# V's weights in whole rows by contraction blocks, and a new order of the first V projections, in a one-core attention and gated-MLP kernel

## The chip, the cores and the metric

The kernel runs on one core of a Trainium2 chip. The metric is the device time of one execution in microseconds. The time is the median of the runs; beside it stands one execution that was taken with the hardware profiler, from which all rows and durations come.

## The reference

One input x (2048 rows of 640) goes through a layer norm, and the normalised rows feed two branches whose results are added to x:

```python
xn = _layernorm(x)
# A: 32 heads of 20, a causal window of 256
qkv = (xn @ wqkv).reshape(B, S, 3, H, Dh)          # wqkv: 640 x 1920
scores = einsum("bhqd,bhkd->bhqk", q, k) * Dh**-0.5
p = softmax(where(0 <= i - j < 256, scores, -1e9))
A = (p @ v) @ wo                                    # wo: 640 x 640
# B: a gated unit
Bo = (sigmoid(xn @ w_gate) * (xn @ w_up)) @ w_down  # 640 x 1536, 1536 x 640
return x + A + Bo
```

All tensors are bfloat16.

## The kernel before

The 2048 rows are worked in four chunks of 512 rows, each of four blocks of 128 (`s` is the block in the chunk, 0 to 3). The 640 features are five contraction blocks of 128 (`d`, 0 to 4). A normalised block is turned (rows to columns) so that the features lie on the partitions, in `xnT`. Everything after the first V projections runs from an order written out by hand: TensorE is fed with scores and with pieces of the other matmuls from a list. The change touches only the start, chunk 0, up to the first matmul of Q.

**Transfers at the start.** They all go out on SP's queue, in program order: the blocks 0, 1 and 3 of x, the first half of V's weights, block 2 of x, the second half of V's weights, then Q's, K's and the gated unit's weights. V's weights are the last 640 columns of `wqkv`, held in SBUF as `wqkv[2]`, 128 partitions by 5 contraction blocks by 640. A half is 320 columns of all five contraction blocks, so each row that it reads in HBM is 640 bytes. A DMA runs on 16 DMA engines, and its reader waits for the last of them.

**Layer norm of the first four blocks.** `ln_block` (bn_stats on two halves, then the aggregate, L252 and L258) with `root` (ACT's square root, L649) and `norm` (DVE's reciprocal L653 and normalisation L271) is the way over DVE. `mean_act`, `root_act` and `norm_act` (L659, L664, L665, L669, L670) take the mean and the squares on ACT, and only the last two small steps on DVE. Before, blocks 0 and 3 go over DVE, blocks 1 and 2 over ACT.

**Transposes.** `transpose_rows(s, copy)` has TensorE transpose a block's five 128 x 128 squares into one PSUM buffer `pt` (L277), and `copy` (ACT's or DVE's) brings them to `xnT[0]` (L278). Block 0 is copied by ACT in two pieces, contraction blocks 0 to 2 and 3 to 4.

**V.** `project_v(c, s, hf)` sums five matmuls of 128 x 320 (L353) into a PSUM buffer `pv`: block s, half hf of V's columns. Its name below is `v` with s and hf: `v10` is block 1, first half. `between` is a function that is called after the third matmul, which puts other work for TensorE there. `copy_v` brings a finished sum to the V tile in two copies (L364), by ACT or by DVE; `proj_v` does both. There are two PSUM pools of four buffers each: `ps_d` (sums) and `ps_h` (transposes, and block 3's two sums).

**Keeping TensorE busy.** `keep_busy` (L226) issues matmuls of ones that nobody reads.

Each engine works through its instructions in program order, so the order of the calls in the start section (L673 to L711) is the order on TensorE, ACT and DVE. After V come the five blocks of Q and the five of K (`g_qk(0)`, L324), and the gated unit's and scores' matmuls. Q's results leave PSUM by DVE, K's by ACT (L328, L330).

Of the kernel before, what the change touches and what calls it, by code (L numbers as in the profile page):

```python
# [9 lines left out]
P = 128  # L10
S = 2048
D = 640
# [3 lines left out]
DC = D // P  # L16
FC = F // P
CW = 512
# [7 lines left out]
HALF = 320  # L26
# [12 lines left out]
FP32 = mybir.dt.float32  # L39
# [54 lines left out]
def kernel(  # L94
# [11 lines left out]
    nc = tc.nc  # L106
# [4 lines left out]
    def pool(name, bufs, **kw):  # L111
        return ctx.enter_context(tc.tile_pool(name=name, bufs=bufs, **kw))
# [15 lines left out]
    ps_d = pool("ps_d", 4, space=bass.MemoryType.PSUM)  # L128
    banks = ctx.enter_context(ExitStack())
    ps_h = banks.enter_context(tc.tile_pool(name="ps_h", bufs=4, space=bass.MemoryType.PSUM))  # L130
# [11 lines left out]
    wqkv = [const.tile([P, DC + (part != "v"), D], BF16, name="w" + part) for part in "qkv"]  # L142
    wqkv_r = A_wqkv.rearrange("(c p) n -> p c n", p=P)
# [6 lines left out]
    def load_wqkv(part):  # L150
        nc.sync.dma_start(out=wqkv[part][:, 1:, :], in_=wqkv_r[:, :, part * D:(part + 1) * D])
# [3 lines left out]
    def load_rows(s, queue):  # L155
        queue.dma_start(out=xc[0][:, s, :], in_=xr[:, s, :])  # L156

    def load_v(hf):
        a = hf * HALF
        nc.sync.dma_start(out=wqkv[2][:, :, a:a + HALF], in_=wqkv_r[:, :, 2 * D + a:2 * D + a + HALF])  # L160

    load_rows(0, nc.sync)
    load_rows(1, nc.sync)
    load_rows(3, nc.sync)
    load_v(0)
    load_rows(2, nc.sync)
    load_v(1)
    load_wqkv(0)
    load_wqkv(1)

# [78 lines left out]
    def ln_half(c, s, a, stats=None):  # L249
        if a == 0:  # L250
            stats = lnp.tile([P, 2, nc.vector.BN_STATS_DIM], FP32, name="stats")
        nc.vector.bn_stats(out=stats[:, a, :], in_=xc[c][:, s, a * HALF:(a + 1) * HALF])  # L252
        return stats

    def ln_mv(stats, mv=None):
        if mv is None:
            mv = lnp.tile([P, nc.vector.BN_AGGR_DIM], FP32, name="mv")
        nc.vector.bn_aggr(out=mv, in_=stats)  # L258
        return mv

    def ln_block(c, s, mv=None):
        return ln_mv(ln_half(c, s, 1, ln_half(c, s, 0)), mv)
# [7 lines left out]
    def norm_block(c, s, mv, rstd):  # L270
        nc.vector.tensor_scalar(out=xns[c][:, s, :], in0=xc[c][:, s, :], scalar1=mv[:, 0:1],  # L271
                                scalar2=rstd[:, 0:1], op0=SUB, op1=MULT)

    def transpose_rows(s, copy, lo=0, hi=DC):
        pt = ps_h.tile([P, DC, P], BF16, name="pt", tag="h")
        for d in range(lo, hi):
            nc.tensor.transpose(pt[:, d, :], xns[0][:, s, d * P:(d + 1) * P], ident)  # L277
        copy(out=xnT[0][:, lo:hi, s * P:(s + 1) * P], in_=pt[:, lo:hi, :])  # L278
# [68 lines left out]
        nc.gpsimd.memset(v[:, :, 0:16 * VW].rearrange("p k (h d) -> p k h d", d=VW)[:, :, :, DH:VW], 0.5)  # L347
        nc.gpsimd.memset(v[:, :, 16 * VW:], 0.0)

    def project_v(c, s, hf, home=ps_d, tag="d", between=None):  # L350
        ps = home.tile([P, CW], FP32, name="pv", tag=tag)
        for d in range(DC):
            nc.tensor.matmul(ps[:, 0:HALF], lhsT=xnT[c][:, d, s * P:(s + 1) * P],  # L353
                             rhs=wqkv[2][:, d, hf * HALF:(hf + 1) * HALF],
                             start=(d == 0), stop=(d == DC - 1))
            if between and d == 2:
                between()
        return ps

    def copy_v(c, s, hf, ps, copy, us=(0, 1)):  # L360

        v = vt[c * SBC + s][hf * U:(hf + 1) * U, :, 0:16 * VW].rearrange("p k (h d) -> p k h d", d=VW)
        for u in us:
            copy(out=v[:, u, :, 0:DH],  # L364
                 in_=ps[u * U:(u + 1) * U, 0:HALF].rearrange("p (h d) -> p h d", d=DH))

    def proj_v(c, s, hf, copy):
        copy_v(c, s, hf, project_v(c, s, hf), copy)
# [278 lines left out]
    def root(mv):  # L647
        r = lnp.tile([P, 1], FP32, name="rstd")
        nc.scalar.activation(out=r, in_=mv[:, 1:2], func=SQRT, bias=eps)  # L649
        return r  # L650

    def norm(s, mv, r):
        nc.vector.reciprocal(r, r)  # L653
        norm_block(0, s, mv, r)

    def mean_act(s):
        xn = xns[0][:, s, :]
        neg = lnp.tile([P, 1], FP32, name="neg")
        nc.scalar.activation(out=xn, in_=xc[0][:, s, :], func=IDENTITY, scale=-1.0 / D, accum_out=neg)  # L659
        return xn, neg  # L660

    def root_act(s, xn, neg):
        r = lnp.tile([P, 1], FP32, name="rstd")
        nc.scalar.activation(out=xn, in_=xc[0][:, s, :], func=SQUARE, bias=neg, accum_out=r)  # L664
        nc.scalar.activation(out=r, in_=r, func=SQRT, bias=eps, scale=1.0 / D)  # L665
        return r

    def norm_act(s, xn, neg, r):
        nc.vector.reciprocal(r, r)  # L669
        nc.vector.tensor_scalar(out=xn, in0=xc[0][:, s, :], scalar1=neg[:, 0:1],  # L670
                                scalar2=r[:, 0:1], op0=ADD, op1=MULT)
# [5 lines left out]
    act, dve = nc.scalar.copy, nc.vector.tensor_copy  # L677
# [8 lines left out]
    keep_busy((CW, P))  # L686
    norm_act(1, xn1, neg1, r1)
    mv3 = ln_mv(ln_half(0, 3, 1, stats3))
    transpose_rows(1, dve)
    v00 = project_v(0, 0, 0)  # L690
    r3 = root(mv3)
    xn2, neg2 = mean_act(2)
    r2 = root_act(2, xn2, neg2)
    norm(3, mv3, r3)
    v10 = project_v(0, 1, 0)
    copy_v(0, 0, 0, v00, dve, (0,))
    transpose_rows(3, dve)
    v01 = project_v(0, 0, 1)
    norm_act(2, xn2, neg2, r2)
    copy_v(0, 0, 0, v00, act, (1,))  # L700
    copy_v(0, 1, 0, v10, act)
    v11 = project_v(0, 1, 1)
    copy_v(0, 0, 1, v01, act)
    v30 = project_v(0, 3, 0, ps_h, "h", lambda: transpose_rows(2, dve))
    copy_v(0, 3, 0, v30, act)
    v31 = project_v(0, 3, 1, ps_h, "h")
    copy_v(0, 1, 1, v11, dve)
    copy_v(0, 3, 1, v31, act)
    proj_v(0, 2, 0, dve)
# [75 lines left out]
    c = NCH - 1  # L785
# [64 lines left out]
```

## Time and profile before

| what | us |
|---|---|
| median of 3 runs (307.92 to 308.11) | 308.0 |
| the profiled execution | 308.12 |
| its span | 306.4 |
| TensorE's granted clock, share of full | 1.00 |
| V's first matmul (L353) starts | 7.10 |
| Q's first matmul (L324) starts | 13.09 |

The span is the time from the first to the last instruction that the profile shows; the execution's own time has 1.7 us more around it. Times in the timeline and in the chain are microseconds from the start of the span. A line of the timeline is a start, a length, the engine, the line of the kernel, the operation, what it writes and reads with its shape, how many instructions are merged, and in brackets the idle time ahead of it with what ended it. PE is TensorE, PEld its weight loads, DVE VectorE, ACT ScalarE, POOL GpSimd, SPq the queue that issues DMAs.

### The profile page before, as it was taken

The numbers are of one execution on the slowest core, as the hardware profiler recorded it, in microseconds if no ns is written. First come the engines' busy times: TensorE is split into PE (matmuls) and PEld (weight loads), VectorE is DVE, ScalarE is ACT, GpSimd is POOL, SyncE is SP. The second block draws the span as 40 slices with busy tenths as digits, with TensorE's granted clock in tenths as the row PEclk, the third lists the DMA queues.
The fourth block names the chain that finished last, engine by engine and source line by source line (L and its number), as shares of the span: only waits on it lengthen the run. The fifth ranks groups of instructions, "written<-read, shape, count | busy, mean of one in ns | idle before, by whom it ended". The sixth has DMA issues, their size and how long they took to land.

```text
span 306.4 us, 10016 instructions
## 1 busy us (share of the span) xinstructions
PE 299.8 (98%) x4290; PEld 165.4 (54%) x4325; DVE 177.6 (58%) x355; ACT 199.2 (65%) x198; POOL 177.0 (58%) x317
## 2 busy tenths in 40 slices
PE   7999999999999999999999999999999999999996
PEld 3654444445657654554557654554546665444775
DVE  5735539879675564496946464483733626372434
ACT  6933877698854649888674647878585547778000
POOL 3174687687982927676682728557382847657000
PEclk9999999999999999999999999999999999999999
DMA  7997977886427052810046212740000210000202
GB/s 204 364 328 259 300 201 220 313 242 203 156 90 171 21 181 68 263 50 2 2 132 131 66 58 71 249 142 0 2 2 2 68 43 25 2 2 2 88 21 68
DMA packets 40174, 36.87 MB, mean 120 GB/s; under 512 B 8864, under 2 KB 39840, under 8 KB 40096
## 3 DMA queue, kind: packets, MB, share of 16 engines
q1 hardware_dynamic: 39264, 35.46, 37.6%
q10 hardware_dynamic: 864, 0.75, 0.8%
q8 instruction: 34, 0.56, 0.7%
q14 instruction: 12, 0.10, 0.1%
HBM read 25.59 MB, written 11.44 MB: 121 GB/s over the span
## 4 chain that ended last, share of the span: by engine, by line
PE 96%; DMA 2%; issue 1%; SPq 0%; ACT 0%; ACTq 0%; DVE 0%
PE y L472 18%; PE pu L456 17%; PE pg L449 17%; PE pqk L324 14%; PE ps L529 9%; PE pv L353 7%; PE y L480 7%; PE acc L562 6%; DMA wv<-in_A_wqkv_dram 2%; SPq L156 0%; ACT th L821 0%; PE pt L277 0%; ACTq L496 0%; DVE xn L484 0%
## 5 line engine op out<-in xcount | busy, mean ns | idle before, releaser
L546 POOL TENSOR_SCALAR_AFFINE_SELECT pT<-pT 64x512 bf16<-64x512 bf16 (+1 forms) x256 | 157.0, 613 | 83.4 <-ACT pT L535 71.0
L535 ACT ACTIVATE pT<-ps 128x2048 bf16<-128x2048 f32 (+1 forms) x76 | 141.0, 1855 | 59.4 <-PE ps L529 58.7
L460 DVE SCALAR_TENSOR_TENSOR h<-th,pu 128x512 bf16<-128x512 f32 x48 | 32.7, 680 | 49.8 <-PE pu L456 44.2
L456 PE MATMUL pu<-xnT,wu 128*128 128x512 bf16 x228 | 59.0, 380 | 0.7 <-issue 0.2
L449 PE MATMUL pg<-xnT,wg 128*128 128x512 bf16 x226 | 58.5, 380 | 1.0 <-issue 0.3
L472 PE MATMUL y<-wd,h 128*128 128x320 bf16 (+3 forms) x407 | 56.6, 292 | 0.0
L472 PEld LDWEIGHTS <-h 128*128 128x128 bf16 x407 | 37.1, 98 | 15.3 <-issue 1.8
L452 ACT ACTIVATE th<-pg 128x512 f32<-128x512 f32 x48 | 28.6, 595 | 15.5 <-PE pg L449 15.4
L449 PEld LDWEIGHTS <-wg 128*128 128x128 bf16 x240 | 22.2, 98 | 25.8 <-issue 1.8
L456 PEld LDWEIGHTS <-wu 128*128 128x128 bf16 x240 | 22.0, 98 | 25.5 <-issue 2.0
L529 PE MATMUL ps<-qT,kT 20*64 20x320 bf16 (+4 forms) x1440 | 32.1, 260 | 0.0
L574 DVE STREAM_TRANSPOSE t<-acc 128x512 f32<-128x512 f32 x32 | 21.1, 697 | 17.3 <-PE acc L562 17.3
L529 PEld LDWEIGHTS <-kT 20*64 20x64 bf16 x1440 | 15.4, 103 | 25.0 <-issue 22.4
L484 DVE SCALAR_TENSOR_TENSOR rows<-y,rows 128x320 bf16<-128x320 f32 x30 | 14.5, 487 | 22.9 <-PE y L480 22.7
L586 DVE TENSOR_TENSOR on<-t,rec 128x320 bf16<-128x320 f32 (+4 forms) x48 | 26.0, 542 | 1.1
L353 PE MATMUL pv<-wv,xnT 128*128 128x320 bf16 x160 | 25.6, 300 | 0.1
L480 PE MATMUL y<-wo,oc 128*128 128x320 bf16 (+2 forms) x165 | 24.2, 295 | 0.0
L324 PE MATMUL pqk<-xnT,wk 128*128 128x512 bf16 x97 | 23.0, 380 | 0.2
L324 PE MATMUL pqk<-xnT,wq 128*128 128x512 bf16 x94 | 22.7, 380 | 0.4 <-issue 0.2
L364 DVE CAST v<-pv 64x320 bf16<-64x320 f32 x29 | 14.1, 485 | 11.7 <-PE pv L353 11.4
L562 PE MATMUL acc<-pT,v 64*32 64x320 bf16 (+4 forms) x1440 | 19.7, 253 | 0.0
L562 PEld LDWEIGHTS <-v 64*32 64x32 bf16 x1440 | 16.2, 91 | 5.8 <-issue 1.6
(54 smaller groups left out, 195.4 us busy)
## 6 DMA issues: line engine op xcount, KB each, us to landing
qT<-sq SPq DMA_DIRECT2D x16, 256.0 KB
kT<-sk SPq DMA_DIRECT2D x16, 256.0 KB
sq<-st SPq DMA_DIRECT2D x20, 128.0 KB
sk<-st SPq DMA_DIRECT2D x20, 128.0 KB
out_dram<-rows SPq DMA_DIRECT2D x15, 160.0 KB
wg<-in_B_w_gate_dram SPq DMA_DIRECT2D x4, 480.0 KB
wu<-in_B_w_up_dram SPq DMA_DIRECT2D x4, 480.0 KB
xc<-in_A_x_dram SPq DMA_DIRECT2D x3, 640.0 KB
```

The costliest lines, as they stand in the source:

```text
L324: nc.tensor.matmul(ps, lhsT=wt[:, m, :], rhs=xnT[c][:, d, :], start=(d == 0), stop=(d == DC - 1))
L353: nc.tensor.matmul(ps[:, 0:HALF], lhsT=xnT[c][:, d, s * P:(s + 1) * P], rhs=wqkv[2][:, d, hf * HALF:(hf + 1) * HALF], start=(d == 0), stop ...
L449: nc.tensor.matmul(pg, lhsT=part(wg, d, f), rhs=xnT[c][:, d, :], start=(d == 0), stop=(d == DC - 1))
L452: nc.scalar.activation(out=th, in_=pg, func=TANH, scale=0.5)
L456: nc.tensor.matmul(pu, lhsT=part(wu, d, f), rhs=xnT[c][:, d, :], start=(d == 0), stop=(d == DC - 1))
L460: nc.vector.scalar_tensor_tensor(out=h, in0=th, scalar=1.0, in1=pu, op0=ADD, op1=MULT)
L472: nc.tensor.matmul(y[:, lo:lo + width], lhsT=ht[c, f][:, s * P:(s + 1) * P], rhs=wd[:, f, cut[0] + lo:cut[0] + lo + width], start=(f == 0) ...
L480: nc.tensor.matmul(y[:, 0:cut[1] - cut[0]], lhsT=oc[c, m][:, s * P:(s + 1) * P], rhs=wo[:, m, cut[0]:cut[1]], start=False, stop=(m == DC - 1))
L529: nc.tensor.matmul(ps[a * U:(a + 1) * U, i, col * U:(col + n) * U], lhsT=qk["k", kc, o // GH][32 * i:32 * i + DH, o % GH + a, kb * U:(kb + ...
L535: nc.scalar.activation(out=pt[:, :, 0:width], in_=ps[:, :, 0:width], func=EXP, scale=SCALE)
L546: nc.gpsimd.affine_select(out=view, in_=view, pattern=[[0, HG], [0, n], [sign, U]], compare_op=GE, fill=0.0, base=base, channel_multiplier ...
L562: nc.tensor.matmul(acc[32 * i:32 * i + 32, q * U:(q + n) * U], lhsT=vt[kb][a * U:(a + 1) * U, u, h * VW:h * VW + 32], rhs=pt[a * U:(a + 1) ...
```

## The change

V's weights are loaded as contraction blocks 0 to 2 and then 3 to 4, each in whole rows of 640 columns (1280 bytes), and block 2 of x follows both pieces. TensorE begins both sums of block 0 before either is complete: three matmuls of `v00` come ahead of block 1's transposes, three of `v01` behind them, then the remaining two of each. Block 3's transposes stand after two matmuls of `v10` and are copied by ACT. Block 2's layer norm goes over DVE (`ln_block`, `root`, `norm`), its transposes stand after one matmul of `v31`. ACT takes both copies of `v00`. All of V's sums and all copies are still made once.

```diff
-    def load_v(hf):
-        a = hf * HALF
-        nc.sync.dma_start(out=wqkv[2][:, :, a:a + HALF], in_=wqkv_r[:, :, 2 * D + a:2 * D + a + HALF])
+    def load_v(lo, hi):
+        nc.sync.dma_start(out=wqkv[2][:, lo:hi, :], in_=wqkv_r[:, lo:hi, 2 * D:])
...
-    load_v(0)
+    load_v(0, 3)
+    load_v(3, DC)
     load_rows(2, nc.sync)
-    load_v(1)
...
-    def project_v(c, s, hf, home=ps_d, tag="d", between=None):
-        ps = home.tile([P, CW], FP32, name="pv", tag=tag)
-        for d in range(DC):
+    def add_v(ps, c, s, hf, lo, hi):
+        for d in range(lo, hi):
             nc.tensor.matmul(ps[:, 0:HALF], lhsT=xnT[c][:, d, s * P:(s + 1) * P],
                              rhs=wqkv[2][:, d, hf * HALF:(hf + 1) * HALF],
                              start=(d == 0), stop=(d == DC - 1))
-            if between and d == 2:
-                between()
+
+    def project_v(c, s, hf, home=ps_d, tag="d", between=None, at=0):
+        ps = home.tile([P, CW], FP32, name="pv", tag=tag)
+        add_v(ps, c, s, hf, 0, at)
+        if between:
+            between()
+        add_v(ps, c, s, hf, at, DC)
         return ps
...
+    v00 = ps_d.tile([P, CW], FP32, name="pv", tag="d")
+    v01 = ps_d.tile([P, CW], FP32, name="pv", tag="d")
+    add_v(v00, 0, 0, 0, 0, 3)
     transpose_rows(1, dve)
-    v00 = project_v(0, 0, 0)
+    add_v(v01, 0, 0, 1, 0, 3)
+    add_v(v00, 0, 0, 0, 3, DC)
+    add_v(v01, 0, 0, 1, 3, DC)
     r3 = root(mv3)
-    xn2, neg2 = mean_act(2)
-    r2 = root_act(2, xn2, neg2)
     norm(3, mv3, r3)
-    v10 = project_v(0, 1, 0)
-    copy_v(0, 0, 0, v00, dve, (0,))
-    transpose_rows(3, dve)
-    v01 = project_v(0, 0, 1)
-    norm_act(2, xn2, neg2, r2)
-    copy_v(0, 0, 0, v00, act, (1,))
+    mv2 = ln_block(0, 2)
+    copy_v(0, 0, 0, v00, act)
+    v10 = project_v(0, 1, 0, between=lambda: transpose_rows(3, act), at=2)
+    r2 = root(mv2)
+    v11 = project_v(0, 1, 1)
+    norm(2, mv2, r2)
+    copy_v(0, 0, 1, v01, act)
     copy_v(0, 1, 0, v10, act)
-    v11 = project_v(0, 1, 1)
-    copy_v(0, 0, 1, v01, act)
-    v30 = project_v(0, 3, 0, ps_h, "h", lambda: transpose_rows(2, dve))
+    v30 = project_v(0, 3, 0, ps_h, "h")
+    v31 = project_v(0, 3, 1, ps_h, "h", lambda: transpose_rows(2, dve), 1)
     copy_v(0, 3, 0, v30, act)
-    v31 = project_v(0, 3, 1, ps_h, "h")
     copy_v(0, 1, 1, v11, dve)
     copy_v(0, 3, 1, v31, act)
     proj_v(0, 2, 0, dve)
     proj_v(0, 2, 1, act)
```

## The prediction

> **What bounds the kernel now.** I read the page first (shares, then the chain), then the chain in order of time, then the timeline of the first 16 us engine by engine, then the packet and completion records of the first transfers.
>
> The page's first part and its chain:
>
> ```profile
> PE 299.8 (98%) x4290; PEld 165.4 (54%) x4325; DVE 177.6 (58%) x355; ACT 199.2 (65%) x198; POOL 177.0 (58%) x317
> PE 96%; DMA 2%; issue 1%; SPq 0%; ACT 0%; ACTq 0%; DVE 0%
> ```
>
> TensorE carries 96% of the chain. The one other piece of size is a DMA, 2%. The chain in order of time (start, length, what) shows where that lies:
>
> ```profile
> 2.18 4.88 DMA wv<-in_A_wqkv_dram
> 7.06 0.04 issue
> 7.10 1.52 PE pv L353 x10
> 8.62 0.28 PE pt L277 x5
> 8.90 1.77 PE pv L353 x13
> 10.66 0.28 PE pt L277 x5
> 10.94 2.31 PE pv L353 x17
> 13.25 0.21 PE pqk L324
> ```
>
> The first half of V's weights lands at 7.06 us; from 7.10 TensorE runs without a hole until Q's first matmul starts at 13.09 (the timeline's figure; the chain books it later since matmuls overlap). That stretch is 40 matmuls of V at 0.136 (5.43) and 10 transposes at 0.056 (0.56): 5.99 us, no stall in it. After it TensorE stays packed to the end, so whatever moves Q's first matmul moves the end by as much, and nothing after V in this diff can win time. The timeline gives what surrounds it (start, length, engine, line):
>
> ```profile
> 5.77 0.75 ACT L278 COPY xnT<-pt 128x384 bf16<-128x384 bf16 x2
> 6.53 0.45 PE L277 MATMUL pt<-ident,xn 128*128 128x128 bf16 x5 [0.41 <-DVE xn L670]
> 7.04 0.48 DVE L278 COPY xnT<-pt 128x640 bf16<-128x640 bf16 x1
> 7.48 0.16 DVE L653 RECIPROCAL rstd<-rstd 128x1 f32<-128x1 f32 x1
> 7.68 0.45 DVE L271 TENSOR_SCALAR xn<-xc,mv,rstd 128x640 bf16<-128x640 bf16 x1
> 9.64 4.79 ACT L364 CAST v<-pv 64x320 bf16<-64x320 f32 x11
> 10.98 0.49 DVE L278 COPY xnT<-pt 128x640 bf16<-128x640 bf16 x1 [0.68 <-PE pt L277]
> ```
>
> To be seen: block 1's transposes (6.53) are done while TensorE still waits for the weights, so they cost nothing now; a transposed block is copied 0.48 after its transposes start; block 0's first three columns are in SBUF at 6.25 (first of the two ACT copies, 5.77 to 6.25), its last two at 6.52.
>
> **The change, part by part.** I write S for the start of V's first matmul, L for the landing of the first weight piece (S = L + 0.04, as 7.06 to 7.10; not below 6.30, the 6.25 of ACT's copy plus 0.05).
>
> *The weight pieces.* Before: 400 KB as 640 packets of 640 bytes, 40 on each of 16 DMA engines. After: 480 KB as 384 packets of 1280 bytes, 24 on each. In the packet records one engine's 640-byte packets follow each other every 28 ns, its 1280-byte packets every 52 ns. So pure streaming is 40 x 28 = 1.12 before and 24 x 52 = 1.25 after: the wide rows are no shorter. The rest is waiting. The block loaded just before (rows of block 3) completes on its 16 engines between 3.78 and 4.08; the first half of V's weights between 5.37 and 7.06, with 5.8 in the middle. On the last engine that is 2.98 us, 1.12 of streaming and 1.86 of waits; single packets took 786 ns (at 3.64) and 1216 ns (at 4.45) instead of 32. What waits the new piece meets is the one unknown that decides. Upper end: the same 1.86, L = 4.08 + 1.25 + 1.86 = 7.19. Middle: waits in proportion to packets, 1.86 x 24/40 = 1.12, L = 6.45. Lower end: the waits that the 1280-byte pieces of x show, whose engines complete within 0.33 of each other (2.75 to 3.08 for the first), L = 5.66, which the copy's floor makes 6.26. The long packets stand mostly among the first quarter of the piece, which speaks against full proportion; the x rows, the nearest of this packet size, speak for less. I take L = 6.7, S = 6.74.
>
> The Trainium skill (DMA: Bandwidth & Descriptors, Latency and other measured facts) gives HBM's access latency as 0.2 us on average and 2 us at high load, that is, by load and not by packet size. The trace's long packets (786, 1216 ns) lie inside that. By that rule alone the waits would stay and L would be the 7.19 of the upper end.
>
> *The second piece*, 320 KB, 16 packets an engine: 16 x 52 = 0.83 after the first, 7.53, plus waits of its own of 0 to 0.5 (the second half of before, 7.49 to 8.61 on the last engine, had none: 1.12 is its streaming). It is needed at S + 1.09 = 7.83. Hidden unless its waits pass 0.3; up to 0.43 they lie under the wait below.
>
> *Block 2 of x* goes one place back on SP's queue, behind the second piece: landing 7.53 + 8 x 52 ns = 7.95, to 8.45. Its reader is now DVE's bn_stats at S + 1.90 = 8.64. Hidden. The number of DMAs on SP stays, at about 0.43 of issue each; Q's weights (10.87 before, wanted at 13.09) stay hidden.
>
> *TensorE's order.* Three V matmuls (0.41) stand ahead of block 1's transposes. TensorE works in order, so those five transposes now wait for the weights too: they move from idle time onto the path, +0.28 (5 x 0.056). Then, from S: block 1's transposes start at 0.41 and end at 0.69; three matmuls to 1.09; four with the second piece to 1.64; two of block 1 to 1.91.
>
> *DVE and block 3.* DVE's copy of block 1 starts at 0.41 + 0.48 = 0.89. Behind it queue, as before, the reciprocal (+0.44), the normalisation (+0.20, 0.45 long) and then block 3's transposes (+0.06): S + 2.04. TensorE is there at 1.91: stall 0.13. Before, the same chain ended at 8.13 and TensorE came at 8.46.
>
> *ACT.* It loses block 2's mean and square passes (7.51 to 9.62) and gains block 3's copy. That copy, 640 wide, is in no row: 0.49 by DVE's row, 0.75 by ACT's two pieces together; ACT's 384 (0.480) and 256 (0.378) extrapolate to 0.68, which I take. Block 0's V copies (2 x 0.43) precede it, from 1.55 to 2.42; the copy runs 2.52 to 3.20. TensorE wants block 3's columns at 2.04 + 0.28 + 0.41 + 0.68 = 3.41: hidden, with 0.75 too. Two sums of V are begun at once; both their PSUM buffers are free from the start.
>
> *Block 2.* bn_stats twice and the aggregate on DVE end at S + 3.02 (0.41, 0.51, 0.21 behind the normalisation); the root on ACT follows block 3's copy, to 3.42; reciprocal and normalisation end at 4.10; transposes can start at 4.16. TensorE, after v30's five and one of v31, is there at 4.22: no stall. But the copy of block 2 then needs 0.48 + 0.49 + 0.05 = 1.02 from 4.22, and TensorE has only five transposes and four matmuls to do (0.28 + 0.54 = 0.82): stall 0.20 ahead of v20. Before, seven matmuls stood there.
>
> *Sum.* Q starts at S + 5.43 + 15 x 0.056 + 0.13 + 0.20 = S + 6.60, against S + 5.99. With S = 6.74: 13.34, +0.25 us. Break-even is S = 6.49. ACT's V copies and the table load end some 0.4 later relative to S (8.64 behind S before); ACT's next customer is at 19.77, so that is hidden. The profiled execution took 308.12 (span 306.4): 308.37; the median of the runs is 0.12 lower: 308.25.
>
> **The rivals.**
>
> *Slower: the transposes behind a late piece.* If the wide piece's last engine waits as long as now, L = 7.19, S = 7.23 and Q starts at 13.83: +0.74, 308.75. The 0.28 of transposes and the 0.33 of stalls are paid and nothing is won. With a second piece that waits 0.6 it is 0.2 more, 308.95. It passes the 0.2% bound (0.62 us, about what a measurement of this kernel can tell from no change) from S = 7.11. For it: long packets sit at the piece's start, whatever its size, and the slowest of 16 engines counts. Against: 256 fewer packets to be hit. The rule of the Trainium skill named above is this rival's.
>
> *Early: weights no longer the wait.* If waits are as in the x pieces, S = 6.30 by ACT's copy, Q at 12.90: -0.19, 307.8. Even with both stalls gone it is 12.58, -0.51, still inside 0.2%; that is the floor of the change. For it: packets of this size in x meet only short waits. Against: 1.86 of waits now, and x's rows lie close together in HBM where V's lie 3840 bytes apart.
>
> *The wait moves to the second piece.* If the 1.86 fall on contraction blocks 3 and 4, whose rows only the second piece reads: 4.08 + 1.25 + 0.83 + 1.86 = 8.02, wanted at 7.39 to 7.83. Q then starts at 8.06 + 6.60 - 1.09 - 0.13 = 13.44: +0.35, 308.35.
>
> **How the numbers follow.** Forecast (L 6.45 to 7.05, -0.0 to +0.6) 0.42; slower rival 0.33; early 0.15; second piece 0.10. The first, third and fourth lie within 0.2%, less 0.05 for a gain outside the floor that I do not see: faster 0.05, same 0.62, slower 0.33. The range goes from the early case, 307.8, into the slower one, 308.9.
>
> **What would show it.** Right: V's first matmul near 6.74, from the first piece's landing; block 1's transposes behind three of V's; a gap of about 0.13 ahead of block 3's and of 0.20 ahead of v20, and Q's first near 13.34. Wrong: a first matmul at 7.1 or later (slower), or at 6.30 released by ACT (early); a gap ahead of V's fourth contraction block names the second piece; a hole after 13.3 or a TensorE clock below the 1.00 of now would break the step that V's shift is the end's shift.

## The result and the profile after

The changed kernel takes 308.70 us (median of 15 runs, 308.28 to 309.79), the kernel before 308.02 (15 runs on the same chips, 307.84 to 308.49): +0.68 us, ratio 1.0023 with a 95% interval of 1.0014 to 1.0032. That interval straddles the 0.2% bound of the prediction: a small loss at the edge of what can be told. The changed kernel also scatters more (1.5 us against 0.65).

The profiled execution took 309.18 us, its span 307.3. It lies 0.48 above its own median, so its excess over the profile of before (1.06) is not the change's price but one draw of it. The page's engines:

```profile
PE 300.0 (98%) x4290; PEld 165.3 (54%) x4325; DVE 178.2 (58%) x356; ACT 198.4 (65%) x196; POOL 176.6 (57%) x317
```

The page counts the same 4290 matmuls on TensorE, still at 98%. ACT has two instructions fewer, DVE one more. The chain in order of time (start, length, what) shows the front:

```profile
2.18 4.94 DMA wv<-in_A_wqkv_dram
7.12 0.04 issue
7.16 0.57 PE pv L351 x3
7.73 0.28 PE pt L276 x5
8.01 1.22 PE pv L351 x9
9.23 0.37 PE pt L276 x5
9.60 1.90 PE pv L351 x14
11.50 0.28 PE pt L276 x5
11.78 0.56 PE pv L351 x4
12.34 0.03 issue
12.37 1.53 PE pv L351 x10
13.90 0.22 PE pqk L323
```

The first weight piece lands at 7.12 in this execution, 0.06 later than the half did before. Then come three matmuls of V, block 1's transposes, nine matmuls, block 3's transposes, 14 matmuls, block 2's transposes, four matmuls, a hole, ten matmuls. The timeline (start, length, engine, line; in brackets idle time and what ended it) gives the two stalls:

```profile
7.16 0.57 PE L351 MATMUL pv<-wv,xnT 128*128 128x320 bf16 x3 [1.07 <-DMA wv<-in_A_wqkv_dram]
9.14 0.28 PEld L276 LDWEIGHTS <-xn 128*128 128x128 bf16 x5 [0.25 <-DVE xn L270]
9.64 0.69 ACT L277 COPY xnT<-pt 128x640 bf16<-128x640 bf16 x1
11.82 0.49 DVE L277 COPY xnT<-pt 128x640 bf16<-128x640 bf16 x1 [0.62 <-PE pt L276]
12.36 1.20 PEld L351 LDWEIGHTS <-xnT 128*128 128x128 bf16 x10 [0.37 <-DVE xnT L277]
13.74 2.54 PE L323 MATMUL pqk<-xnT,wq 128*128 128x512 bf16 x10
```

Block 3's transposes wait for DVE's normalisation (0.08 more between starts than the usual 0.136), v20 for DVE's copy of block 2 (0.34 between starts, 0.20 more than usual). Q's first matmul comes at 13.74, 6.58 behind V's first; before it was 13.09, 5.99 behind.

The 1.06 us between the two profiled executions fall as follows: V's first matmul +0.06; from it to Q's +0.59; two later gaps of TensorE +0.10 (the larger, 0.08, at 58.4 us); from the start of the last matmul to the end of the span +0.18 (2.79 before, 2.97 after); outside the span +0.13.

### The profile page after: what moved, and what is told of

It reads as the page before. It is cut to its first block, busy times and chain, and to the rows that moved or that the text cites. A ratio compares the mean times of both kernels' runs of the same rounds, so it can differ in the third digit from the quotient of the medians.

```text
span 307.3 us, 10014 instructions
## 1 busy us (share of the span) xinstructions
PE 300.0 (98%) x4290; PEld 165.3 (54%) x4325; DVE 178.2 (58%) x356; ACT 198.4 (65%) x196; POOL 176.6 (57%) x317
## 4 chain that ended last, share of the span: by engine, by line
PE 96%; DMA 2%; issue 1%; SPq 0%; ACT 0%; ACTq 0%; DVE 0%
PE y L475 18%; PE pu L459 17%; PE pg L452 17%; PE pqk L323 14%; PE ps L532 9%; PE pv L351 7%; PE y L483 7%; PE acc L565 6%; DMA wv<-in_A_wqkv_dram 2%; SPq L156 0%; PE pt L276 0%; ACT th L826 0%; ACTq L499 0%; DVE xn L487 0%
## 5 line engine op out<-in xcount | busy, mean ns | idle before, releaser
L351 PEld LDWEIGHTS <-xnT 128*128 128x128 bf16 x160 | 14.7, 98 | 9.7 <-issue 1.6
```

## The experiments

What had to be told apart was why the first piece lands when it does (size, packets, the distance of its rows in HBM, or chance), whether the order of TensorE's work costs what the sum said, and where the rest of the median's +0.68 is. Below, S is V's first matmul, Q is Q's first, L the landing of the first weight piece on its last engine, and the tail is the time from the start of the last matmul to the end of the span.

**load_only.** The kernel before with the new weight pieces alone, TensorE's order the old one.

```
-    load_v(0)
+    load_v(0, 3)
+    load_v(3, DC)
     load_rows(2, nc.sync)
-    load_v(1)
```

> The kernel before with only its loads changed: V's weights in contraction blocks 0-2 and 3-4, whole rows, block 2 of x behind both; every engine's order is the old one. Theory A (the order of the work costs, the pieces land no earlier): V's first matmul near 7.1 as before, the first sum then waits ahead of its fourth contraction block for the second piece (7.95 in the changed kernel's profile), about 0.45 us; block 2 of x lands near 8.4 instead of 7.49, so block 2's transposes wait some 0.25 more; Q starts near 13.8, about +0.7 us on the kernel before. Rival B (the whole-row pieces do land earlier in most runs, the changed kernel's profile being a late one): first matmul near 6.7, Q near 13.4, +0.3.

Measured: 308.57 us (308.39 to 309.24), ratio 1.0016 [1.0007, 1.0024]. L 6.59, S 6.77, Q 13.37. Chain, in order of time:

```profile
3.18 4.72 DMA xc<-in_A_x_dram
7.90 0.02 issue
7.92 0.84 ACT xn L658 x2
...
10.78 0.45 PE pt L276 x5
11.23 2.31 PE pv L352 x17
13.54 2.59 PE pqk L323 x12
```

The chain starts with block 2 of x and not with the weights: one place further back on SP's queue it lands at 7.90, ACT's passes over it follow, and TensorE stands 0.27 longer than usual ahead of its transposes. Another 0.34 goes ahead of the fourth contraction block, whose second piece (7.47) is wanted earlier in the old order. S came 0.33 earlier than in the profile of before, and all of it and 0.28 more was lost again. So the new pieces ask for the new order, in which block 2 is read later and a second sum is begun with the first three contraction blocks.

**turn_first.** The changed kernel with block 1's transposes ahead of V's first matmul again.

```
-    add_v(v00, 0, 0, 0, 0, 3)
     transpose_rows(1, dve)
+    add_v(v00, 0, 0, 0, 0, 3)
```

> The changed kernel with block 1's transposes put back ahead of V's first three matmuls; nothing else differs. Theory A (those transposes moved from idle time onto the path): they run at 6.5 again, DVE's copy of block 1 starts at 7.0, block 3's transposes find their rows ready, Q starts 6.2 us after V's first matmul instead of 6.58: -0.36 us on the changed kernel, and +0.2 to +0.3 on the kernel before at the same landing. Rival B (the loss is the landing of the weights alone): Q still about 6.58 behind V's first matmul, or a new wait in place of the old, time as the changed kernel's (+0.68 on before).

Measured: 308.37 us (308.20 to 309.21), ratio 1.0011 [1.0002, 1.0019]; 0.33 less than the changed kernel. Its profiled execution met a late piece:

```profile
2.18 5.53 DMA wv<-in_A_wqkv_dram
7.71 0.04 issue
7.75 1.82 PE pv L351 x12
9.57 0.28 PE pt L276 x5
```

Q lies 6.23 behind S instead of 6.58: the 0.28 of transposes and the stall ahead of block 3's are gone, the one ahead of v20 (0.34 between starts) is left. The part of the change that puts three matmuls ahead of block 1's transposes costs a third of a microsecond in the trace (0.34). The medians differ by as much, but their intervals overlap.

**other_rows.** The changed kernel with the first pieces read from the contiguous rows of another tensor of the same size (V's own weights are left out).

```
-        nc.sync.dma_start(out=wqkv[2][:, lo:hi, :], in_=wqkv_r[:, lo:hi, 2 * D:])
+        nc.sync.dma_start(out=wqkv[2][:, lo:hi, :], in_=wo_r[:, lo:hi, :])
```

> The changed kernel with V's weights read from wo instead of from the last 640 columns of wqkv: as many packets of 1280 bytes, but rows that lie one behind the other in HBM instead of 3840 bytes apart (so it multiplies by the wrong weights). It asks what the long packets come from. Theory C (from the rows' distance): the first piece lands by 6.2, V's first matmul at 6.30 released by ACT's copy, Q near 12.9, -0.2 us on the kernel before. Rival D (from the early phase of the transfers, whatever they read): landing near 7.1 with long packets as before, +0.65 on the kernel before.

Measured: 308.48 us (308.28 to 310.10), ratio 1.0019 [1.0007, 1.0031]. L 6.66, S 6.70, Q 13.27. Six profiles of the 480 KB piece from V's own rows have L 7.12, 6.34, 6.59, 7.71, 6.84 and 6.69; 6.66 is one of them. The landing by 6.2 that was expected if the distance of 3840 bytes between V's rows were the cause did not come. One profile, beside a scatter of 1.4 us, does not exclude a smaller effect.

**three_pieces.** The changed kernel with the 480 KB cut into two of 240 (contraction blocks 0 to 2 of one half of the columns, then of the other).

```
-    load_v(0, 3)
+    load_v(0, 3, 0, HALF)
+    load_v(0, 3, HALF, D)
     load_v(3, DC)
```

> The changed kernel with V's weights in three pieces: contraction blocks 0-2 of the first half (24 packets of 640 bytes an engine), the same of the second half, then blocks 3-4 in whole rows. If the waits stand at the start of the first piece whatever its size (theory E): landing 4.08 + 0.67 + 1.86 = 6.6, first matmul 6.64; the third piece at 8.1 then holds V's fourth contraction block back by about 0.3, Q near 13.5, +0.4 us on the kernel before. If the waits go with the packets (rival F): landing near 5.9, first matmul 6.30 released by ACT's copy, and the third piece decides: Q 13.0 to 13.5, -0.1 to +0.4.

Measured: 308.82 us (308.15 to 310.00), ratio 1.0026 [1.0013, 1.0039]. The pieces land at 5.83, 6.57 and 8.00. S is 6.43, released by ACT's copy at 6.37: with a smaller first piece V's first matmul no longer waits for the weights. But the third piece is now late, and the chain starts with it:

```profile
3.19 4.81 DMA wv<-in_A_wqkv_dram
8.00 0.04 issue
8.04 0.97 PE pv L352 x6
```

Q is at 13.43, 7.00 behind S. The profiled execution of 310.0 has one more loss, seen in the chain much later:

```profile
82.68 1.47 PE y L476 x10
84.14 0.88 issue
85.02 2.06 PE y L476 x14
```

At that place the kernels before and after run 24 matmuls without a break; the line of the timeline of before is

```profile
82.27 3.43 PE L472 MATMUL y<-wd,h 128*128 128x320 bf16 x24
```

In the packet records one packet of 16 KB, about 1 us long, on a queue that carries instructions lies there. In before it starts at 80.23, 2.04 ahead of the first of the 24 matmuls; here at 82.72, 0.11 behind the first (82.61). That it holds TensorE's next instructions is inferred; the last section has the other profiles.

**two_copies.** turn_first, and block 2's transposed columns copied out as 3 + 2, so that the copy starts behind the third transpose.

```
-    v31 = project_v(0, 3, 1, ps_h, "h", lambda: transpose_rows(2, dve), 1)
+    v31 = project_v(0, 3, 1, ps_h, "h", lambda: (transpose_rows(2, dve, 0, 3), transpose_rows(2, dve, 3, DC)), 1)
```

> turn_first, and block 2's transposes and DVE's copy of them in two pieces (contraction blocks 0-2, then 3-4), as block 0's are. Theory A (V's tail: a whole copy takes 1.02 us where TensorE has 0.82 of work): v20's first matmuls start on the first piece, the gap of 0.34 between matmuls ahead of v20 (0.20 over the usual 0.136) goes, Q starts 6.03 us after V's first matmul instead of 6.23: -0.2 us on turn_first, within 0.1 of the kernel before at the same landing. Rival: two small copies cost DVE more than they hide, the gap moves to v20's fourth matmul, no gain.

Measured: 308.64 us (308.06 to 309.41), ratio 1.0021 [1.0011, 1.0031]. In the trace both stalls are gone: S 6.88, Q 12.88, 6.00 apart, as in the kernel before. The profiled execution took 308.35 all the same: its tail is 3.23 instead of 2.79. The median is no better than the changed kernel's, and the gain of 0.2 on turn_first that was expected did not come.

**four_sums.** Three pieces, block 1's transposes first, then the first three contraction blocks of four sums (v00, v01, v10, v11), block 3's transposes, and the last two contraction blocks of the four; block 2's copy in two.

```
+    transpose_rows(1, dve)
+    first = [(s, hf, ps_d.tile([P, CW], FP32, name="pv", tag="d")) for s in range(2) for hf in range(2)]
+    for s, hf, ps in first:
+        add_v(ps, 0, s, hf, 0, 3)
...
+    transpose_rows(3, act)
+    for s, hf, ps in first:
+        add_v(ps, 0, s, hf, 3, DC)
```

> Three pieces as in three_pieces, block 1's transposes first, then the first three contraction blocks of all four sums of blocks 0 and 1 (twelve matmuls, 1.63 us), block 3's transposes with ACT's copy ahead of block 0's V copies, then the last two contraction blocks of the four sums, and block 2 in two copies. Theory A (order and landing are two separate costs, the first piece of 240 KB lands near 5.8, and the third near 8.0 to 8.5 is wanted only at 8.67): V's first matmul at 6.76 behind block 1's transposes, no wait for weights at all, Q 6.0 to 6.1 behind it, near 12.8: -0.2 to -0.3 us on the kernel before and the runs closer together. Rival: the wait comes back in block 2's chain, behind ACT's copies, 0.2 or more, and nothing is won.

Measured: 308.50 us (308.14 to 309.06), ratio 1.0012 [1.0003, 1.0020]. Its chain:

```profile
6.47 0.45 PE pt L277 x5
6.92 1.63 PE pv L352 x12
8.55 0.28 PE pt L277 x5
8.84 1.90 PE pv L352 x14
10.74 0.28 PE pt L277 x5
11.02 1.90 PE pv L352 x14
12.92 0.22 PE pqk L324
```

No weight piece is on the chain (they land at 5.97, 6.63 and 7.51) and TensorE has no hole. Q starts at 12.75, the earliest of all, 0.34 ahead of before. The profiled execution took 308.51: the tail is 3.32 (+0.53), and a gap of 0.19 stands at 83.2 us. The gain of 0.2 to 0.3 on the kernel before that was expected did not come.

**before_again, after_again.** The two kernels once more, one profile each.

> The kernel before once more, for a second sample of the landing of V's first half. If a 400 KB piece of 640-byte packets lands steadily: last engine within 0.2 of 7.06, V's first matmul 7.0 to 7.2. If its landing scatters as the whole-row pieces' does (6.59, 7.12 and 7.71 so far): anywhere from 6.6 to 7.7.

> The changed kernel once more, for another sample of the landing of the first whole-row piece. Theory A: Q again 6.58 behind V's first matmul whatever the landing, which lies from 6.6 to 7.7; the time is Q's start plus 295.0 to 295.4 us. A Q further from V's first matmul would mean a second piece that is late by more than the first.

Measured: before 308.00 with L 6.65, S 6.80 (here block 1's transposes end last), Q 12.88, tail 2.80; after 308.20 with L 6.34, S 6.38, Q 12.96, tail 2.96. The distance from S to Q repeats (6.07 with S set by the transposes, and 6.58), so does the tail. The landing does not: 0.41 and 0.78 earlier than in the first profiles. One landing is no base for a forecast of a few tenths.

**after_two_act.** The changed kernel with two one-column activations more on ACT behind V, which gives ACT as many instructions as before.

```
     nc.scalar.activation(out=scr, in_=neghalf[:, 0:1], func=EXP)
+    nc.scalar.activation(out=scr, in_=neghalf[:, 0:1], func=EXP)
+    nc.scalar.activation(out=scr, in_=neghalf[:, 0:1], func=EXP)
```

> The changed kernel with two more one-column activations on ACT, in its idle time after V, so that ACT again has 198 timed instructions as the kernel before. In every kernel with the new order ACT's first drain at the end takes 628 ns and a second one 141 ns, and the span ends 2.96 to 2.98 us after the last matmul starts, against 2.79 to 2.80 in the kernel before and load_only, whose second to last program fetch comes 1.9 us after that matmul instead of 3.3. Theory G (the end depends on where ACT's instructions lie in the stream that is fetched): 2.79 again, -0.17 us on the changed kernel, with V as it was. Rival H (the end comes from the stores or from DVE): 2.97 as in the changed kernel.

Measured: 308.70 us (308.17 to 311.04), ratio 1.0023 [1.0005, 1.0041]. In the trace the tail is back at 2.80, and the drain that closes ACT's program takes 350 ns, as before, where the changed kernel has 628 and 141. The changed kernel's longer tail is this second drain: GpSimd's closing steps end at 306.94 there, as long behind the last matmul as before (2.57 and 2.56), and its next step comes at 307.16, behind the drain's end at 307.13; before, it came 0.05 behind them. Two idle instructions take the drain away, so it hangs on ACT's stream of instructions and not on its work. But 0.12 is lost near 84 us, and the median did not move; its interval, half a microsecond to either side, can't tell 0.17.

**four_sums_pad.** four_sums with those two activations and eight one-column memsets on DVE.

```
+    idle = const.tile([P, 1], FP32, name="idle")
+    for _ in range(8):
+        nc.vector.memset(idle, 0.0)
```

> four_sums (Q at 12.75, 0.34 us earlier than in the kernel before, but the span ended 3.32 us after the last matmul's start instead of 2.79, with a program fetch at 303.2 among the last stores) with two more one-column activations on ACT and eight one-column memsets on DVE, all in their idle time after V, so that the fetches fall elsewhere. Theory G: the tail returns to 2.8, Q stays near 12.75, -0.2 to -0.3 us on the kernel before (307.75 to 307.85). Rival H: the tail stays at 3.3 and the time at 308.4 to 308.5.

Measured: 308.26 us (307.94 to 309.09), ratio 1.0006 [0.9993, 1.0018]: the best of the variants, not to be told from the kernel before. The tail is 2.88, Q 12.95 (block 2 of x landed at 8.54 and held its transposes), and TensorE loses 0.45 at 83.4 us.

**before_one_dve.** The kernel before with one such memset.

> The kernel before with one more one-column memset on DVE, in its idle time after V. Theory G: DVE's count is then that of two_copies (one more), the program fetch that stood at 305.2 comes about 2 us earlier, among the last stores, and the tail grows from 2.79 by some 0.25: 308.3 although nothing else has changed. Rival H (the tail comes from V's new order itself): 2.79, 308.05.

Measured: 308.15 us (307.91 to 308.46), ratio 0.9999 [0.9988, 1.0010]. In the trace one instruction of no use lengthens the tail from 2.79 to 3.08, and the profiled execution takes 308.41. The median rises by 0.07 only, against 0.25 expected. The interval reaches 0.31 us, so whether the tail of a profile is carried over into the times is left open.

**two_and_three.** four_sums_pad with two pieces only: contraction blocks 0 and 1 in whole rows (320 KB), then 2 to 4 (480 KB); the four sums are begun with two contraction blocks instead of three.

```
-    load_v(0, 3, 0, HALF)
-    load_v(0, 3, HALF, D)
-    load_v(3, DC)
+    load_v(0, 2)
+    load_v(2, DC)
```

> A version meant to beat both: two pieces only (contraction blocks 0-1, 320 KB, then 2-4, whole rows), block 1's transposes first, the first two contraction blocks of four sums, block 3's transposes, the other three of the four sums, block 2 in two copies, and four_sums_pad's ten small instructions for the tail. With two pieces SP's transfers keep the count of the kernel before, where the kernels with three pieces met a TensorE gap near 83 us (0.19, 0.50 and 1.04 us) behind a program fetch of 16 KB that started at 81.1 to 82.7 instead of 80.2 to 80.7. If order and landing are all (theory A): V's first matmul at 6.76 behind block 1's transposes, the second piece at 7.6 to 8.2 holds TensorE by 0 to 0.3, Q at 12.8 to 13.1, tail 2.8: -0.3 to 0.0 us on the kernel before, 307.8 to 308.1. Rival J (what is won at the start is given back at a late program fetch): Q as early, but a TensorE gap near 83 us that takes it back, 308.2 to 308.5.

Measured: 308.62 us (308.02 to 308.74), ratio 1.0011 [1.0002, 1.0020]. Chain:

```profile
2.66 6.09 DMA wv<-in_A_wqkv_dram
8.75 0.04 issue
8.79 2.60 PE pv L351 x18
11.39 0.44 PE pt L276 x5
```

The first piece lands at 5.90 and holds nobody (S 6.77, behind block 1's transposes). The second lands at 8.75, and Q comes 6.80 behind S. Ahead of it TensorE had already stood 0.27, for block 1's columns (7.52) and block 3's transposes (8.14), which two contraction blocks don't cover; the wait for the piece itself is 0.36, and block 2 of x (landed at 9.16) costs 0.15 more. This is the prediction's rival in which the wait moves to the second piece; the changed kernel, with three of five contraction blocks in its first piece, does not have it, and this cut does.

**All profiles in one sum.** From the profile of before (308.12) each profiled time follows from Q, the gaps of TensorE after it, and the tail:

| kernel | S | Q | gaps later | tail | sum | profiled | median |
|---|---|---|---|---|---|---|---|
| before | 7.10 | 13.09 | 0 | 2.79 | 308.12 | 308.12 | 308.02 |
| after | 7.16 | 13.74 | 0.10 | 2.97 | 309.05 | 309.18 | 308.70 |
| load_only | 6.77 | 13.37 | 0 | 2.79 | 308.40 | 308.40 | 308.57 |
| turn_first | 7.75 | 13.99 | 0 | 2.98 | 309.21 | 309.21 | 308.37 |
| two_copies | 6.88 | 12.88 | 0 | 3.23 | 308.35 | 308.35 | 308.64 |
| four_sums | 6.76 | 12.75 | 0.19 | 3.32 | 308.50 | 308.51 | 308.50 |
| four_sums_pad | 6.79 | 12.95 | 0.50 | 2.88 | 308.57 | 308.59 | 308.26 |
| after_two_act | 6.73 | 13.31 | 0.12 | 2.80 | 308.47 | 308.48 | 308.70 |
| two_and_three | 6.77 | 13.57 | 0.08 | 2.78 | 308.67 | 308.69 | 308.62 |
| three_pieces | 6.43 | 13.43 | 1.04 | 3.07 | 309.78 | 310.00 | 308.82 |
| other_rows | 6.70 | 13.27 | 0 | 2.96 | 308.47 | 308.48 | 308.48 |
| before_one_dve | 7.08 | 13.07 | 0 | 3.08 | 308.39 | 308.41 | 308.15 |
| before_again | 6.80 | 12.88 | 0 | 2.80 | 307.92 | 308.00 | one run |
| after_again | 6.38 | 12.96 | 0.02 | 2.96 | 308.18 | 308.20 | one run |

The sum (308.12, plus the differences of Q, gaps and tail to the first row) meets the profiled time within 0.02 in ten of the thirteen rows below the first. In the other three (off by 0.08, 0.13 and 0.22) 0.08 to 0.13 lies outside the span. What the traces do not give is the median of a kernel: two_copies has Q 0.21 earlier than before in its profile and a median 0.59 later than before's 308.05 in that comparison, of which the profile's longer tail would be 0.44.

## Why the prediction was right, and where its working was not

The forecast was 308.25 in a range of 307.8 to 308.9, with a small loss below the bound as the likeliest outcome. The measured 308.70 lies inside, in the range's upper half. It is 0.45 above the forecast and 0.05 from the 308.75 of the slower rival: the change cost 0.68 where 0.25 was forecast, and it was the range, drawn into that rival, that held it. Point by point:

- **TensorE's order: right.** From V's first matmul to Q's 6.60 was forecast and 6.58 measured, in three profiles alike (after, after_again, after_two_act). The transposes on the path are 0.28 as said (turn_first takes them off, and 0.07 of the stall with them). The stall ahead of v20 is 0.20 as forecast, the one ahead of block 3's transposes 0.08 instead of 0.13. Taken together they are 0.56 of the +0.59 that is the larger part of the loss.
- **ACT's copy of 640 columns: right.** 0.68 was extrapolated, 0.69 measured, hidden as said.
- **The second piece and block 2: right.** They land at 7.95 and 8.40 in the changed kernel's first profile (readers at 8.25 and 9.01, as S was 7.16). load_only and two_and_three show that the new order is the cover: without it the same transfers cost 0.6, and two_and_three, with a larger second piece, loses 0.8, of which 0.5 stands at the second piece and at block 2.
- **The landing of the first piece: the term that was mis-sized.** The step "I take L = 6.7" was near the mark as a value (mean of the six profiles 6.88). The fault was to set it against the one 7.06 of the profile of before, as a gain of 0.36. Three profiles of the old half give 7.06, 6.65 and 7.04, mean 6.92: by the means whole rows win 0.04, not 0.36. S gains 0.07 by the same means (6.99 before, since block 1's transposes can hold it; 6.92 after). Three and six landings that scatter by 0.4 and 1.4 us do not exclude a few tenths, but the medians leave little room: with the order at 0.59 and the tail at 0.17, the changed kernel's +0.68 leaves a gain of 0.08, and turn_first's +0.31, with 0.24 and 0.18, one of 0.11, each give or take 0.3. The base of the sum was as single: block 3's rows landed at 4.08 in the profile of before, but between 4.78 and 5.07 in twelve of the fourteen, in after_again (4.98) with the earliest 480 KB piece of all. So L less 4.08 was not the wait of the piece alone, and rows of 1280 bytes meet long waits too.
- **The end of the program: a term that was missing.** "Whatever moves Q's first matmul moves the end by as much" left out the time behind TensorE's end: the tail grows by 0.17, ACT's second drain.

With these two put right the sum is -0.07 + 0.59 + 0.17 = +0.69, and the medians differ by +0.68. That agreement is closer than its parts deserve, and in part luck: the landings scatter by over 1 us, against the mean of the old kernel's three profiles (6.02 from S to Q) the order costs 0.56, and before_one_dve and after_two_act moved the tail of the profile without moving the median. Shown, in the traces, is the 0.59: it repeats, turn_first takes 0.34 of it away and two_copies all of it. That whole rows win next to nothing rests on means and medians. That the last 0.17 of the median is the tail is argued.

The slower rival (L 7.19) was right for the executions with a late piece, as the first profile after. By the means it was the nearer account altogether: the whole rows land as late as the half did, so nothing is won, and transposes and stalls are paid. The early rival was nearly met once, in after_again (S 6.38), which took 308.20 and still did not beat the kernel before. Between the chances of 0.33 for a loss over 0.2% and 0.62 within it a ratio of 1.0023 [1.0014, 1.0032] does not decide.

The Trainium skill (DMA: Bandwidth & Descriptors, Latency and other measured facts) gives HBM's access latency by load, 0.2 us on average and 2 us at high load. By that rule alone the piece's wait would stay the same whatever its size. Here it is in between. Less their streaming the pieces land at 5.2 (240 KB, mean of three), 5.07 (320 KB, one profile), 5.80 (400 KB, mean of three) and 5.63 (480 KB, mean of six): the two smaller sizes wait some 0.6 less, and within each pair the larger piece does not wait longer.

The Trainium skill (DMA: Bandwidth & Descriptors, Why a DMA increments its semaphore by 16 and not by 1) says that the engines of a transfer finish independently and that only the full count of 16 means that all data have landed. The trace agrees: the first piece of the changed kernel completes on its 16 engines between 5.49 and 7.12, on half of them by 5.9, and TensorE starts 0.04 after the last one.

What stays open: how much of a profile's tail is in the times, and with it why the medians of two_copies and four_sums are not below before's, though in their profiles Q is earlier. In four_sums the profiled execution (308.51) is the median, and tail and gap account for it. In two_copies the median lies 0.29 above the profiled execution, and its scatter (308.06 to 309.41) asks for a cause that one profile doesn't show. No variant beat the kernel before.

## What to carry to other kernels

Where a kernel waits at its start for the slowest of 16 engines, the landing is a distribution: take it from several profiles before pricing a change against it, and remember that a smaller first piece moved it here (5.9 against 6.9) while wider rows did not. Work that stands in idle time ahead of such a wait (here five transposes) is free only there; moved behind the wait's end it is paid in full, whenever the data come. And a piece's cut and the order that reads it are one decision: the new cut in the old order gave back the 0.33 us by which its profile started earlier, and 0.28 more.

## What was not expected of the hardware

- **Loading of the program is seen in TensorE's time.** What counts is how far the 16 KB packet starts ahead of the 24 matmuls that three_pieces broke up (82.27 in before). In nine of the fourteen profiles that lead is 1.35 to 2.17 us, and the 24 run without a break, in turn_first too, whose packet starts as late as 81.49. At a lead of 1.01 (after_again) they take 0.02 longer. At leads of 0.88, 0.83 and 0.46, and where the packet starts 0.11 late (four_sums, after_two_act, four_sums_pad, three_pieces), TensorE loses 0.19, 0.12, 0.45 and 1.04, each time behind the tenth of the 24 matmuls. The burst of data packets went on until 81.06, 82.25, 81.73 and 82.72 in these four, and until 80.57 in before. That the packet holds TensorE's instructions and that the burst delays it goes with these numbers and wasn't tested by itself.
- **The tail hangs on the instruction streams.** The last instruction that the timeline shows, a cast on ACT, starts at 304.50 before and 305.25 after and takes 0.62 us in both. From its end the span of before ends 1.3 us later, that of after 1.5. Over all profiles the tail runs from 2.78 to 3.32, and one memset of a single column on DVE moved it by 0.29.
